# Two added ordering rules in a spectral layer with a feed-forward behind it, on one core: a segment's products behind a gate, and the down matmuls behind the next unit's gate

## The chip, the cores and the metric

The kernel runs on 1 core of one Trainium2 chip. The metric is the device time of one execution in microseconds (us), lower is better. In the profile the engines are PE (TensorE's matmuls), PEld (its weight loads), DVE (VectorE), ACT (ScalarE), POOL (GpSimd) and SP (which issues the DMAs).

## The reference

The input is x of 8 batches of 3008 positions by 256 channels. A Fourier layer is followed by a feed-forward layer over all 8 x 3008 = 24064 positions:

```
X = np.fft.rfft(x, axis=1)
Yr = Xr @ w_r - Xi @ w_i + b_r
Yi = Xr @ w_i + Xi @ w_r + b_i
Yr, Yi = soft threshold of both at 0.01
y = np.fft.irfft(Yr + 1j * Yi, n=3008, axis=1)
...
h = y.reshape(24064, 256) @ w_in          # 256 x 2048
g = h * np.clip(h + 3.0, 0.0, 6.0) / 6.0
out = g @ w_out                           # 2048 x 256
```

## The kernel before

**The spectral part.** The transform of 3008 = 64 x 47 points is cut in two. For each batch `stage1` multiplies by the 47-point table (L332), `middle` does the 64-point transforms, the channel mixing with w_r and w_i and the threshold, and the way back (L421, the w_r/w_i/w_m products that go through the helper line L137, L506), and `segment` does the last 47-point products (L558) from `qt`, which a DMA loads. Each batch has seven segments; segment (b, k) writes its part of `raw`, the input of the feed-forward, by two ACT copies (L566) and DVE additions (L568, L580). `prepare(c)` then makes from chunk c of 512 positions the operands `yb`, each split into a high and a low part (L130 on ACT, L131 on DVE or POOL).

**The feed-forward.** There are 47 chunks of 512 positions, and for each one 8 *units* (c, f), each with two of the 16 column blocks of w_in: 376 units, numbered from 0. A unit's product with w_in is done as seven smaller *blocks* instead of eight (a Strassen scheme). A block is three matmuls of 256 columns (low x high, high x low, high x high). They go to three PSUM tiles:

- `pb` (two buffers, so unit i and unit i+2 share one) takes blocks 1, 6, 7 and 4 in this order, one on top of the other. After each block ACT copies the running sum out: `p1`, `u2`, `u3` (L620), and after block 4 `h` (L654). The next block into this buffer has to wait for that copy.
- `pd` (one buffer) takes block 2, `pc` (one buffer) blocks 5 and 3. DVE adds each of them to one of the copies, into `h` (L625).

`phase_a` (blocks 2, 1), `phase_b` (6), `phase_c` (7, 5) and `phase_d` (4, 3) issue them. `gate(i)` is then one ACT activation `r` (L661, the gate's first ACT operation), one DVE operation (L663), the ACT cast that gives the high part of `gs` (L130) and the DVE subtraction that gives the low part (L131). `down(i, step)` issues twelve matmuls of 512 columns in four steps (L685): eight with the high part of `gs`, four with the low part, into `po0` and `po1`, which add up over the 8 units of a chunk. The program issues unit i's blocks, unit i-1's gate and unit i-3's down matmuls in one pass of its loop.

**What sets the order.** The program text gives only a priority. A scheduler goes through the whole program with modelled times when the kernel is built, and fixes the order of each engine's queue: what is ready earlier there can be put ahead of what stands earlier in the text. Each engine then works its queue in that order. Spectral work is spread among the units by `lay(g, n, first, last)`, which puts the n steps of a piece into slots between units `first` and `last`; for segment (b, k) these come from `begin[b, k]`, when its chunk is needed.

Of the kernel before, what the change touches and what calls it, by code (L numbers as in the profile page):

```python
# [13 lines left out]
AF = mybir.ActivationFunctionType  # L14
# [86 lines left out]
def spectral_ffn(ctx: ExitStack, tc: tile.TileContext, x, w_r, w_i, bias, w_in, w_out, f47, f64, g64, sgn, out):  # L101
    nc = tc.nc
# [11 lines left out]
    def space(shape, dt, name, tag=None):  # L114
        tag = tag or name
        return sb.tile(shape, dt, name=name, tag=tag, bufs=depth.get(tag, 1))
# [6 lines left out]
    def room(wide=False):  # L123
        if wide:
            return ps_b.tile([P, 512], F32, name="pb")
        return ps_a.tile([P, 512], F32, name="ps_a")

    def split(hi, lo, src, on=None):

        nc.scalar.copy(out=hi, in_=src)  # L130
        (on or nc.vector).tensor_tensor(out=lo, in0=src, in1=hi.bitcast(F32), op=ALU.subtract)  # L131
# [14 lines left out]
    def loaded(src, rows, cols, name, at=None):  # L146

        hi = const.tile([rows, cols], F32R, name=name + "_hi")
        lo = const.tile([rows, cols], F32R, name=name + "_lo")
        st = const.tile([rows, cols], F32, name=name + "_all") if at is None else at  # L150
        nc.sync.dma_start(out=st[:rows, :cols], in_=src)
        return hi, lo, st[:rows, :cols]
# [5 lines left out]
    nf = NFT // 2  # L158
    three = const.tile([P, 1], F32, name="three")
# [219 lines left out]
    with tc.issue_after(stores[-1].ins):  # L379
        r, k = [loaded(w, P, 2 * D, n, t) for w, n, t in ((w_r, "w_r", spare[7]), (w_i, "w_i", spare[8]))]  # L380
# [149 lines left out]
    def segment(b, k, tag="qt", aside=None):  # L530
        n1, n = SEGS[k]
        gr = 2 if n == 2 * J else 1
        rows = n // gr * NK
        w = n * NK
        t0 = b * S + n1 * N2
        qt = space([P, 2, 2, D], F32, "qt", tag)
        for cs in range(2):
            src = scr2[b][cs, n1 : n1 + n].rearrange("(g j) k d -> (j k) g d", g=gr)
            nc.sync.dma_start(out=qt[:rows, cs, :gr], in_=src)
        for c in range(t0 // T, (t0 + n * N2 - 1) // T + 1):  # L540
            if c not in raw:
                raw[c] = space([P, 2, T], F32, "raw")
        yield

        def places(at, size):

            done = 0
            while done < size:
                c, q = divmod(t0 + at + done, T)
                m = min(size - done, T - q)  # L550
                yield c, q, done, done + m
                done += m

        for dh in range(2):
            ps = room(bool(aside) and dh == 1)
            for cs in range(2):
                for g in range(gr):
                    nc.tensor.matmul(  # L558
                        out=ps[:, cs * w + g * rows : cs * w + (g + 1) * rows],
                        lhsT=qt[:rows, cs, g, dh * P : (dh + 1) * P],  # L560
                        rhs=f47_s[2][:rows, cs * R47 : cs * R47 + rows],
                        start=True,
                        stop=True,
                    )
            odd = space([P, 2 * R47], F32, "odd", aside or "xi")[:, :w]
            nc.scalar.copy(out=odd, in_=ps[:, w : 2 * w])  # L566
            for c, q, lo, hi in places(0, w):
                nc.vector.tensor_tensor(out=raw[c][:, dh, q : q + hi - lo], in0=ps[:, lo:hi], in1=odd[:, lo:hi], op=ALU.add)  # L568

            some = lambda a: a.rearrange("p (n q) -> p n q", q=NK)[:, :, 1:]  # L570
            m = NK - 1
            for c, q, lo, hi in places(w, n * m):
                while lo < hi:
                    row, col = divmod(lo, m)
                    if col == 0 and hi - lo >= m:
                        r1, c1 = hi // m, m
                    else:
                        r1, c1 = row + 1, min(m, col + hi - lo)
                    size = (r1 - row) * (c1 - col)
                    nc.vector.tensor_tensor(  # L580
                        out=raw[c][:, dh, q : q + size].rearrange("p (n q) -> p n q", n=r1 - row),
                        in0=some(ps[:, :w])[:, row:r1, col:c1],
                        in1=some(odd)[:, row:r1, col:c1],
                        op=ALU.subtract,
                    )
                    lo, q = lo + size, q + size
            yield
# [20 lines left out]
            yield  # L608

    units = [(c, f) for c in range(NC) for f in range(nf)]  # L610
    hs, ps_of, keep, gs, pos = {}, {}, {}, {}, {}

    def block(i, n, ps, start):
        c, f = units[i]
# [42 lines left out]
    def gate(i):  # L657

        h = hs.pop(i)
        r = space([P, 2, T], F32, "r")  # L660
        nc.scalar.activation(out=r, in_=h, func=AF.Relu, bias=three, scale=1.0)  # L661
        yield
        nc.vector.scalar_tensor_tensor(out=r, in0=r, scalar=6.0, in1=h, op0=ALU.min, op1=ALU.mult)  # L663
        t = gs[i] = space([P, 2, 2, T], F32R, "gs")
        split(t[:, 0], t[:, 1], r)
        yield
# [6 lines left out]
    )  # L673

    def down(i, step):

        c, f = units[i]
        g = gs[i]
        for u, dh, which, low in STEPS[step]:
            if f == 0 and step < 2 and u == 0 and which == "l":  # L680
                pos[dh] = ps_o.tile([P, 512], F32, name=f"po{dh}")
            part = int(f in shares[1])
            ft = 2 * (f - shares[part][0]) + u
            w = wout_s["hl".index(which)][part]
            nc.tensor.matmul(  # L685
                out=pos[dh],
                lhsT=w[:, ft * D + dh * P : ft * D + (dh + 1) * P],
                rhs=g[:, low, u],
                start=f == 0 and u == 0 and which == "l",
                stop=f == nf - 1 and u == 1 and low == 1,  # L690
            )
            if f == nf - 1 and u == 1 and low == 1:
                ot = space([P, T], F32, "ot")
                if dh:
                    nc.vector.tensor_scalar(out=ot, in0=pos[dh], scalar1=1.0 / 6.0, scalar2=None, op0=ALU.mult)
                else:
                    nc.scalar.mul(out=ot, in_=pos[dh], mul=1.0 / 6.0)
                nc.sync.dma_start(out=out[dh * P : (dh + 1) * P, c * T : (c + 1) * T], in_=ot)
# [16 lines left out]
    with tc.high_priority():  # L715
        for k, tag, aside in ((0, "qt", "p1"), (1, "h", "u2")):
            run(segment(0, k, tag, aside))
        run(prepare(0))
# [4 lines left out]
    def lay(g, n, first, last):  # L723

        q = -1
        for i in range(n):
            q = max(q + 1, int(4 * (first + (last - first) * i / n)))
            while q in taken:
                q += 1
            taken.add(q)  # L730
            slots.setdefault(q, []).append(g)
        return q / 4 + 0.5
# [3 lines left out]
    begin = {}  # L736
    for b in reversed(range(B)):
        for k in reversed(range(len(SEGS))):
            first = 8 * ((b * S + SEGS[k][0] * N2) // T)
# [8 lines left out]
    for b in range(B):  # L748
        for k in range(len(SEGS)):
            if (b, k) not in ((0, 0), (0, 1)):  # L750
                lay(segment(b, k), 3, max(0, begin[b, k]), max(3, begin[b, k] + 3))
        if b:
            lay(middle(b), 3 * (NK // 2) + 2, max(after, per * (b - 1) - 14), begin[b, 0] - 1.5)
        if 0 < b < B - 1:
            after = lay(stage1(b + 1), 29, max(after, per * (b - 1) - 10), max(15, per * b - 16))
# [13 lines left out]
    for i in range(n + 3):  # L769
        for kind, f in ((in_band, i), (out_band, i - 3)):  # L770
            while 0 <= f < nf and (kind, f) not in ready:
                turn(LATE)
        if i < n:
            phase_a(i)
        gated(i - 2)
        fill(4 * i)
        if 0 <= i - 3 < n:
            down(i - 3, 0)
        if 0 <= i - 1 < n:
            phase_c(i - 1)  # L780
        fill(4 * i + 1)
        if 0 <= i - 3 < n:
            down(i - 3, 1)
        if i < n:
            phase_b(i)
        fill(4 * i + 2)
        if 0 <= i - 3 < n:
            down(i - 3, 2)
        if 0 <= i - 1 < n:
            phase_d(i - 1)  # L790
            gates[i - 1] = gate(i - 1)
            gated(i - 1)
        fill(4 * i + 3)
        if 0 <= i - 3 < n:
            down(i - 3, 3)
            gs.pop(i - 3)
# [47 lines left out]
```

## Time and profile before

| | us |
|---|---|
| median of 3 runs | 2629.21 |
| lowest, highest | 2628.64, 2632.96 |
| profiled execution | 2629.63 |
| its span, first to last instruction | 2627.9 |
| PE busy / PEld busy | 2557.6 / 2282.9 |
| DVE / ACT / POOL busy | 1971.7 / 1814.5 / 764.8 |

The profiled execution lies 0.42 us above the median, and 1.7 us of its time lie outside the span. A matmul's bar in the timeline is longer than the distance to the next one's start (0.28 us against 0.12 us for 256 columns), since matmuls are pipelined. So short waits of PE hide under a "busy" bar; the distance of two starts shows them, and the idle time of PEld, whose weight load carries the wait, does too.

### The profile page before, as it was taken

The page shows a single profiled execution, that of the slowest core. Times are in us where ns is not written, and L with a number is a line of the kernel's source. Part 1 is how long each engine was busy: PE and PEld are TensorE (multiplying, and loading weights), DVE is VectorE, ACT ScalarE, POOL GpSimd, SP SyncE. Part 2 cuts the span into 40 slices and gives each one's busy share as a digit, 9 for nine tenths or more (in the row PEclk, how much of TensorE's full clock was granted, in tenths as well). Part 3 has the DMA queues.
Part 4 walks back from the last instruction along what each step waited for, and adds up shares of the span by engine and source line. Part 5 has one row for each costly group of instructions (what it writes and reads, how often), then busy time and mean ns, then how long its engine had stood idle before and what let it go on. Part 6 is the DMA issues. An engine that isn't in the chain of part 4 may idle for free.

```text
span 2627.9 us, 44428 instructions
## 1 busy us (share of the span) xinstructions
PE 2557.6 (97%) x16392; PEld 2282.9 (87%) x16392; DVE 1971.7 (75%) x3195; ACT 1814.5 (69%) x3578; POOL 764.8 (29%) x726
## 2 busy tenths in 40 slices
PE   5789999999999999999999999999999999999999
PEld 4578889988888888998898888988989889888887
DVE  7687777777778777877778777777777777666766
ACT  5477777777767676676766677767776666676666
POOL 3233332333323332333314243233321121131310
PEclk8989999999999999999999999999999999999999
DMA  8643422332123212222223222222222111100000
GB/s 263 186 127 90 114 83 81 88 88 69 56 85 89 78 58 64 87 86 82 62 65 92 74 65 74 80 75 80 66 76 60 48 58 50 41 29 27 12 17 17
DMA packets 149985, 199.97 MB, mean 76 GB/s; under 512 B 16847, under 2 KB 103751, under 8 KB 149767
## 3 DMA queue, kind: packets, MB, share of 16 engines
q1 hardware_dynamic: 149767, 197.13, 25.5%
q8 instruction: 129, 2.11, 0.3%
q14 instruction: 89, 0.73, 0.1%
HBM read 97.45 MB, written 74.97 MB: 66 GB/s over the span
## 4 chain that ended last, share of the span: by engine, by line
PE 84%; DVE 6%; ACT 4%; DMA 2%; issue 1%; SPq 0%; POOL 0%; ACTq 0%; DVEq 0%
PE po L685 37%; PE pb L137 17%; PE ps_a L137 10%; PE pc L137 9%; PE pd L137 4%; PE ps_a L558 3%; PE ps_a L421 2%; ACT gs L130 1%; ACT r L661 1%; DVE r L663 1%; DVE gs L131 1%; DVE h L625 1%; DVE tc L475 0%; DVE tc L474 0%; DMA zt<-tc 0%
## 5 line engine op out<-in xcount | busy, mean ns | idle before, releaser
L685 PE MATMUL po<-gs,w_out_hi 128*128 128x512 f32 x3008 | 1008.6, 396 | 0.0
L663 DVE SCALAR_TENSOR_TENSOR r<-r,h 128x1024 f32<-128x1024 f32 x376 | 486.4, 1294 | 253.2 <-ACT r L661 251.0
L685 PEld LDWEIGHTS po<-gs,w_out_hi 128*128 128x128 f32 x3008 | 540.4, 188 | 84.0
L685 PE MATMUL po<-gs,w_out_lo 128*128 128x512 f32 x1504 | 602.4, 401 | 4.8 <-ACT gs L130 2.3
L137 PE MATMUL pb<-yb,w_in_hi 128*128 128x256 f32 x3008 | 571.3, 279 | 1.3 <-DVE yb L131 1.3
L661 ACT ACTIVATE r<-h,three 128x1024 f32<-128x1024 f32 x376 | 434.7, 1156 | 197.9 <-DVE h L625 195.0
L131 DVE TENSOR_TENSOR gs<-r,gs 128x1024 fp32r<-128x1024 f32 x376 | 486.2, 1293 | 74.0 <-ACT gs L130 72.1
L137 PEld LDWEIGHTS pb<-yb,w_in_hi 128*128 128x128 f32 x3008 | 460.5, 189 | 19.9 <-DVE yb L131 1.6
L130 ACT CAST gs<-r 128x1024 fp32r<-128x1024 f32 x376 | 396.0, 1053 | 97.2 <-DVE r L663 93.8
L625 DVE TENSOR_TENSOR h<-pc,u 128x256 f32<-128x256 f32 x752 | 315.3, 419 | 182.7 <-PE pc L137 168.8
L131 POOL TENSOR_TENSOR yb<-T,yb 128x256 fp32r<-128x256 f32 x184 | 177.7, 971 | 904.8 <-ACT yb L130 870.3
L137 PE MATMUL pb<-yb,w_in_lo 128*128 128x256 f32 x1504 | 430.8, 288 | 5.9 <-ACT yb L130 2.3
L620 ACT COPY u<-pb 128x256 f32<-128x256 f32 x752 | 279.3, 374 | 113.3 <-PE pb L137 96.9
L685 PEld LDWEIGHTS po<-gs,w_out_lo 128*128 128x128 f32 x1504 | 282.7, 188 | 63.0 <-ACT gs L130 13.6
L137 PEld LDWEIGHTS pb<-yb,w_in_lo 128*128 128x128 f32 x1504 | 283.2, 189 | 30.2 <-ACT h L654 4.2
L137 PE MATMUL pc<-yb,w_in_hi 128*128 128x256 f32 x1504 | 296.8, 279 | 0.0
L137 PEld LDWEIGHTS pc<-yb,w_in_hi 128*128 128x128 f32 x1504 | 229.9, 188 | 12.0 <-DVE yb L131 0.3
L137 PE MATMUL pc<-yb,w_in_lo 128*128 128x256 f32 x752 | 218.0, 290 | 1.7 <-DVE h L625 1.5
L620 ACT COPY p<-pb 128x256 f32<-128x256 f32 x376 | 140.1, 373 | 67.4 <-PE pb L137 66.1
L654 ACT COPY h<-pb 128x256 f32<-128x256 f32 x376 | 140.9, 375 | 52.2 <-PE pb L137 51.0
L625 DVE TENSOR_TENSOR h<-pd,p 128x256 f32<-128x256 f32 x376 | 157.0, 418 | 19.4 <-ACT p L620 12.2
L137 PEld LDWEIGHTS pc<-yb,w_in_lo 128*128 128x128 f32 x752 | 141.6, 188 | 16.0 <-DVE h L625 3.5
(139 smaller groups left out, 3878.8 us busy)
## 6 DMA issues: line engine op xcount, KB each, us to landing
bt<-scr SPq DMA_DIRECT2D x96, 256.0 KB, 3.0
scr<-pt SPq DMA_DIRECT2D x96, 256.0 KB, 2.3
zt<-tc SPq DMA_DIRECT2D x376, 64.0 KB, 2.0
out<-ot SPq DMA_DIRECT2D x94, 256.0 KB, 2.3
scr<-a SPq DMA_DIRECT2D x96, 240.0 KB, 2.7
qt<-scr SPq DMA_DIRECT2D x96, 240.0 KB, 3.4
xin<-in_x SPq DMA_DIRECT2D x38, 480.0 KB, 4.5
f<-in_f SPq DMA_DIRECT2D x96, 128.0 KB, 2.8
```

The source lines that it names most:

```text
L130: nc.scalar.copy(out=hi, in_=src)
L131: (on or nc.vector).tensor_tensor(out=lo, in0=src, in1=hi.bitcast(F32), op=ALU.subtract)
L137: nc.tensor.matmul(out=ps, lhsT=a, rhs=b, start=start and n == 0, stop=stop and n == len(todo) - 1, skip_group_check=more,)
L421: nc.tensor.matmul(out=psv[:, dh, :, u, :], lhsT=data[:, u, dh * P : (dh + 1) * P], rhs=f[:, u, :], start=True, stop=True,)
L558: nc.tensor.matmul(out=ps[:, cs * w + g * rows : cs * w + (g + 1) * rows], lhsT=qt[:rows, cs, g, dh * P : (dh + 1) * P], rhs=f47_s[2][:row ...
L620: nc.scalar.copy(out=t, in_=ps)
L625: nc.vector.tensor_tensor(out=to, in0=ps, in1=keep.pop((i, n)), op=ALU.add)
L654: nc.scalar.copy(out=hs[i][:, 1, :H], in_=pb)
L661: nc.scalar.activation(out=r, in_=h, func=AF.Relu, bias=three, scale=1.0)
L663: nc.vector.scalar_tensor_tensor(out=r, in0=r, scalar=6.0, in1=h, op0=ALU.min, op1=ALU.mult)
L685: nc.tensor.matmul(out=pos[dh], lhsT=w[:, ft * D + dh * P : ft * D + (dh + 1) * P], rhs=g[:, low, u], start=f == 0 and u == 0 and which == ...
```

## The change

A function `ordered(later, earlier)` adds a dependency to the scheduler's graph that carries no semaphore (`NoSync`): the order of the queues has to obey it, no engine waits for it. It is used twice.

- The matmuls of the third segment of batch 0, (b, k) = (0, 2), are put behind the first ACT operation of unit 0's gate, and its three steps are laid between units 1.25 and 3.5 instead of 0 and 3.
- From unit 16 on, each down matmul of unit i is put behind the first ACT operation of unit i+1's gate.

```
+    def ordered(later, earlier):
+        why = mybir.DependencyInfo(mybir.DependencyClass.NoSync, mybir.DependencyReason.DATA)
+        tc.add_manual_dep(later.ins, earlier.ins.name, why, reason="order")
...
-                    nc.tensor.matmul(
+                    made_by = nc.tensor.matmul(
...
+                    if (b, k) == (0, 2):
+                        ordered(made_by, gated_by[0])
...
-        nc.scalar.activation(out=r, in_=h, func=AF.Relu, bias=three, scale=1.0)
+        gated_by[i] = nc.scalar.activation(out=r, in_=h, func=AF.Relu, bias=three, scale=1.0)
...
-            nc.tensor.matmul(
+            made_by = nc.tensor.matmul(
                 out=pos[dh],
...
+            if i + 1 in gated_by and i >= 2 * nf:
+                ordered(made_by, gated_by[i + 1])
...
-                lay(segment(b, k), 3, max(0, begin[b, k]), max(3, begin[b, k] + 3))
+                first, last = max(0, begin[b, k]), max(3, begin[b, k] + 3)
+                lay(segment(b, k), 3, *((1.25, 3.5) if (b, k) == (0, 2) else (first, last)))
```

No instruction is added or taken out. In the rows below, the number behind a name tells tiles apart.

PE at the start of the feed-forward, before: qt_1230 is segment (0, 2), pd_1207 and pb_1206 are unit 0.

```order
L558 MATMUL ps_a_1160<-f47_all_90,qt_1156 128x120 x4
L558 MATMUL pb_1170<-f47_all_90,qt_1156 128x120 x4
L558 MATMUL ps_a_1296<-f47_all_90,qt_1230 128x120 x4
L137 MATMUL pd_1207<-yb_1185,w_in_lo_79 128x256
L137 MATMUL pb_1206<-yb_1188,w_in_lo_79 128x256
L558 MATMUL ps_a_1376<-f47_all_90,qt_1230 128x120 x4
L137 MATMUL pb_1272<-yb_1188,w_in_lo_79 128x256
L137 MATMUL pd_1207<-yb_1185,w_in_hi_78 128x256 x2
```

The same place now:

```order
L558 MATMUL ps_a_1160<-f47_all_90,qt_1156 128x120 x4
L558 MATMUL pb_1170<-f47_all_90,qt_1156 128x120 x4
L137 MATMUL pd_1207<-yb_1185,w_in_lo_79 128x256
L137 MATMUL pb_1206<-yb_1188,w_in_lo_79 128x256
L137 MATMUL pb_1268<-yb_1188,w_in_lo_79 128x256
L137 MATMUL pd_1207<-yb_1185,w_in_hi_78 128x256 x2
```

The eight products of segment (0, 2) have gone; they stand some thirty rows later, behind all seven blocks of unit 0, and the first matmuls of `middle(1)` (L421), which stood between unit 0's blocks, stand behind unit 0's first eight down matmuls.

PE late in the program, before: pb_28449 is unit 349, pb_28567 unit 351, which takes the same PSUM buffer; gs_28521 is unit 348.

```order
L137 MATMUL pb_28449<-yb_28042,w_in_lo_79 128x256
L137 MATMUL pb_28449<-yb_28042,w_in_hi_78 128x256 x2
L137 MATMUL pd_28568<-yb_27889,w_in_lo_79 128x256
L137 MATMUL pd_28568<-yb_27889,w_in_hi_78 128x256 x2
L137 MATMUL pc_28530<-yb_28066,w_in_lo_79 128x256
L137 MATMUL pc_28530<-yb_28066,w_in_hi_78 128x256 x2
L685 MATMUL po0_28348<-gs_28521,w_out_lo1_1088 128x512
```

Now (the down matmuls that follow are those of unit 347, gs_28462):

```order
L137 MATMUL pb_28449<-yb_28042,w_in_lo_79 128x256
L137 MATMUL pb_28449<-yb_28042,w_in_hi_78 128x256 x2
L137 MATMUL pb_28567<-yb_27924,w_in_lo_79 128x256
L137 MATMUL pb_28567<-yb_27924,w_in_hi_78 128x256 x2
L137 MATMUL pd_28568<-yb_27889,w_in_lo_79 128x256
L137 MATMUL pd_28568<-yb_27889,w_in_hi_78 128x256 x2
L137 MATMUL pc_28530<-yb_28007,w_in_lo_79 128x256
L137 MATMUL pc_28530<-yb_28007,w_in_hi_78 128x256 x2
L691 MATMUL po0_28348<-gs_28462,w_out_lo1_1088 128x512
```

The down matmuls, which stood in groups of eight and four between the blocks, now stand twelve in a row and one unit later, and the blocks stand closer: the last block of unit 349 in its buffer and the first of unit 351 in the same one, with two blocks, eight down matmuls and one more block between them before, follow each other directly.

ACT at the same place, before: r_28503 and gs_28521 are unit 348, p1_28517 and u2_28546 unit 350, u3_28537 and h_28451 unit 349.

```order
L654 COPY h_28392<-pb_28390 128x256
L620 COPY u2_28487<-pb_28449 128x256
L661 ACTIVATE r_28503<-h_28392,three_75 128x1024
L620 COPY p1_28517<-pb_28508 128x256
L620 COPY u3_28537<-pb_28449 128x256
L130 CAST gs_28521<-r_28503 128x1024
L620 COPY u2_28546<-pb_28508 128x256
L654 COPY h_28451<-pb_28449 128x256
```

Now (r_28444 and gs_28462 are unit 347):

```order
L656 COPY h_28392<-pb_28390 128x256
L622 COPY u2_28487<-pb_28449 128x256
L663 ACTIVATE r_28444<-h_28329,three_75 128x1024
L130 CAST gs_28462<-r_28444 128x1024
L622 COPY p1_28517<-pb_28508 128x256
L622 COPY u3_28537<-pb_28449 128x256
L656 COPY h_28451<-pb_28449 128x256
L622 COPY u2_28546<-pb_28508 128x256
```

The copies `p1` and `u3`, which stood between the gate's two ACT operations, now stand behind both, and `gs` directly behind `r`.

## Rows read from the trace of the kernel before

**Rows 1.** The page's busy time of the engines with their share of the span, its slices of PE and of the granted clock (40 equal slices, tenths), and the engines' shares in the chain that ended last.

```profile
PE 2557.6 (97%) x16392; PEld 2282.9 (87%) x16392; DVE 1971.7 (75%) x3195; ACT 1814.5 (69%) x3578; POOL 764.8 (29%) x726
...
PE   5789999999999999999999999999999999999999
...
PEclk8989999999999999999999999999999999999999
...
PE 84%; DVE 6%; ACT 4%; DMA 2%; issue 1%; SPq 0%; POOL 0%; ACTq 0%; DVEq 0%
```

**Rows 2.** Busy time by stretch (us from the span's start: PE, PEld, DVE, ACT, POOL with instructions; then granted clock as a share of 2.4 GHz, DMA share, GB/s).

```profile
50.00:100.00 50.00, 37.34 (x256) 32.55 (x257) 41.07 (x70) 23.84 (x45) 13.23 (x14) 0.97 0.67 194
140.00:167.00 27.00, 17.30 (x88) 14.87 (x87) 26.42 (x56) 18.98 (x45) 12.54 (x13) 0.75 0.40 121
300.00:2390.00 2090.00, 2079.55 (x13508) 1873.45 (x13507) 1582.41 (x2563) 1467.33 (x2905) 625.90 (x578) 1.00 0.24 71
2390.00:2628.00 238.00, 231.61 (x1441) 205.32 (x1439) 160.15 (x240) 159.35 (x300) 45.18 (x49) 1.00 0.05 17
```

**Rows 3.** The start of the feed-forward in order of time (start us, us, engine line op, out<-in, count, and idle time before it with what released it): segment (0, 2)'s products, unit 0's blocks and the DVE's additions for that segment.

```profile
143.20 1.04 PE L558 MATMUL ps_a<-f_all,qt 120*128 120x120 f32 x4 [2.79 <-DMA qt<-scr]
145.02 1.21 PE L558 MATMUL ps_a<-f_all,qt 120*128 120x120 f32 x4 [0.78 <-DMA qt<-scr]
...
145.89 0.56 PE L137 MATMUL pd<-yb,w_in_lo 128*128 128x256 f32 x1
...
146.46 1.90 PE L558 MATMUL ps_a<-f_all,qt 120*128 120x120 f32 x8
...
147.63 0.23 DVE L568 TENSOR_TENSOR raw<-ps_a,odd 128x84 f32<-128x84 f32 x1
...
152.16 0.51 PE L137 MATMUL pb<-yb,w_in_lo 128*128 128x256 f32 x2 [2.29 <-ACT yb L130]
...
155.43 1.23 PE L137 MATMUL pb<-yb,w_in_hi 128*128 128x256 f32 x4 [1.34 <-DVE yb L131]
...
161.26 1.13 PE L421 MATMUL ps_a<-f,bt 128*128 128x128 f32 x8 [1.16 <-issue]
...
162.14 0.37 PE L137 MATMUL pc<-yb,w_in_lo 128*128 128x256 f32 x1
```

**Rows 4.** Who PE's weight loads waited for from 300 us to the end: us in total, times, longest.

```profile
PEld po L685 <- ACT gs L130: 13.6, 43, 1.2
PEld pb L137 <- ACT h L654: 3.8, 14, 0.3
PEld pb L137 <- ACT p L620: 3.1, 7, 0.9
PEld pc L137 <- DVE h L625: 2.8, 8, 0.5
PEld pd L137 <- DVE h L625: 2.1, 5, 1.0
PEld pb L137 <- ACT u L620: 1.5, 4, 0.7
```

**Rows 5.** One unit's start of a block on a buffer whose copy is not done, at 384 us: block 1, then block 6 of the same unit with only one other matmul's length between them in the order.

```profile
384.08 0.39 PE L137 MATMUL pb<-yb,w_in_hi 128*128 128x256 f32 x2
...
384.51 0.37 ACT L620 COPY p<-pb 128x256 f32<-128x256 f32 x1
...
384.94 0.39 PE L137 MATMUL pb<-yb,w_in_lo 128*128 128x256 f32 x1 [0.46 <-ACT p L620]
```

**Rows 6.** The same at 2040 us, with one block of another unit between: the last block of a unit, the other unit's block, and the first block of the unit that takes the first one's buffer.

```profile
2040.34 0.39 PE L137 MATMUL pb<-yb,w_in_hi 128*128 128x256 f32 x2
...
2040.57 0.28 PE L137 MATMUL pb<-yb,w_in_lo 128*128 128x256 f32 x1
...
2040.77 0.37 ACT L654 COPY h<-pb 128x256 f32<-128x256 f32 x1 [0.57 <-PE pb L137]
...
2041.19 0.38 PE L137 MATMUL pb<-yb,w_in_lo 128*128 128x256 f32 x1
```

**Rows 7.** ACT in one unit's time late in the program, in order of time.

```profile
2469.14 1.16 ACT L661 ACTIVATE r<-h,three 128x1024 f32<-128x1024 f32 x1 [1.15 <-DVE h L625]
2470.20 0.35 ACT L620 COPY u<-pb 128x256 f32<-128x256 f32 x1
2470.44 0.38 ACT L620 COPY p<-pb 128x256 f32<-128x256 f32 x1
2471.58 1.05 ACT L130 CAST gs<-r 128x1024 fp32r<-128x1024 f32 x1 [0.76 <-DVE r L663]
2472.54 0.36 ACT L654 COPY h<-pb 128x256 f32<-128x256 f32 x1
```

**Rows 8.** PE a little later: a block, the eight down matmuls before it, and the same group of the next unit.

```profile
2472.80 0.39 PE L685 MATMUL po<-gs,w_out_lo 128*128 128x512 f32 x1
2473.03 0.40 PE L685 MATMUL po<-gs,w_out_hi 128*128 128x512 f32 x1
...
2474.66 0.28 PE L137 MATMUL pb<-yb,w_in_lo 128*128 128x256 f32 x1
2474.78 0.39 PE L137 MATMUL pb<-yb,w_in_hi 128*128 128x256 f32 x2
2475.01 0.28 PE L137 MATMUL pb<-yb,w_in_lo 128*128 128x256 f32 x1
...
2477.98 0.39 PE L685 MATMUL po<-gs,w_out_lo 128*128 128x512 f32 x1
```

More of the change, by code (lines that the diff above doesn't have):

```diff
@@ L610, in spectral_ffn @@
     units = [(c, f) for c in range(NC) for f in range(nf)]
-    hs, ps_of, keep, gs, pos = {}, {}, {}, {}, {}
+    hs, ps_of, keep, gs, pos, gated_by = {}, {}, {}, {}, {}, {}
     def block(i, n, ps, start):
```

## The prediction

> **What bounds the kernel now.** I read first the page's busy times, slices and chain. PE is busy for 97% of the span, its share of the chain is 84%, and from the seventh slice of forty its slices are full at a granted clock of full speed [rows 1]. No work is taken out, so a time can come only from PE's waits. The stretches say where these lie: from 140 to 167 us PE is busy 17.3 of 27 us, at 0.75 of the clock; from 300 to 2390 us it is busy 2079.55 of 2090 [rows 2]. The second number hides short waits under the bars of pipelined matmuls, so I read next whom the weight loads waited for: of the waits after 300 us the largest item by far is the down matmuls on the cast of `gs`, 13.6 us in 43 waits; the waits of blocks on their copies and additions come to 13.3 us in 38 (3.8 + 3.1 + 2.8 + 2.1 + 1.5) [rows 4]. The change moves down matmuls back, so it is aimed at the first item, and it has to push blocks forward, which is the second.
>
> **Part 1, the third segment.** Before, its first product waits 2.79 and 0.78 us for its DMA while unit 0's first block stands behind it in PE's queue, and the eight products keep PE until 148 us with the clock down [rows 3]. That wait goes. What is late next is `yb`: PE then waits 2.29 us for the ACT cast and 1.34 us for the DVE subtraction [rows 3], and DVE is busy 26.42 of 27 us in this stretch [rows 2]. Only the DVE addition at 147.63 us (0.23 us) leaves that queue ahead of `yb`. Further on, L421 no longer stands in front of unit 0's last block, so PE's 1.16 us wait there and its run of 0.88 us (161.26 to 162.14) go [rows 3]: this block can start at about 162.14 - 1.16 - 0.88 - 0.25 = 159.85 us. But 16 segment passes and 8 of L421, some 0.11 us each at full clock, are then still to do: 2.7 us, so the comparable point is 162.5 us against 162.14. They fill small holes of unit 1's start (under 1 us). I take **-0.5 us**, with -2 and +1 as ends: all of the 2.29 us wait moved away, and nothing filled. On SP's queue the load of segment 3 goes behind two loads of `middle(1)`; its data are for chunk 2, which begins sixteen units in, and I cost that at nothing (a late arrival would cost a wait like the 2.79 us).
>
> **Part 2, the gain.** No wait is added by the rule itself, only order. I counted, for each unit from 17 on, the PE work that stands between the last matmul of its blocks and its first down matmul, a 256-column matmul at 0.116 us and a 512-column one at 0.232 us (2474.66 to 2474.78, 2472.80 to 2473.03) [rows 8]. What must happen in this time is a copy, `r`, a DVE operation and the cast: 0.32 us to the copy [rows 6], then from a late unit's row of ACT about 2.44 us from `r` to `gs` and 0.96 us of `gs`, with the copy and addition ahead some 4.3 us in all [rows 6, 7]. Before, the work between is 4.2 us or less in one unit of twenty and 5.8 us at the median; now it is 6.5 and 7.9 us. So nearly all of the 43 waits should go. Each also costs the first matmul its overlap, about 0.1 us (its bar is 0.39 us, not 0.28) [rows 5]. 13.6 + 4.3 = 17.9 us at most; some small waits on a queue that runs late will stay. I take **-15 us**, ends -18 and -8.
>
> **Part 2, the price.** The same count for blocks that need the copy or addition of an earlier block, over seven such pairs per unit. With no matmul between the two, PE starts the second 0.75 us after the first (the block's last matmul at 384.19, the next at 384.94) instead of 0.12 us [rows 5]; with the lost overlap that is 0.74 us. With one block between, 2040.45 to 2041.19 is again 0.74 us [rows 6], of which 0.47 is work: 0.27 + 0.11 = 0.38 us. With two blocks between, 0.82 us of work cover it and about 0.04 us are left, an estimate from these two rows. Pairs with under 0.3 us of work between: 1 before, 20 now. From 0.3 to 0.6 us: 26 before, 75 now. From 0.6 to 0.9 us: 37 before, 179 now. The difference is 19 x 0.74 + 49 x 0.38 + 142 x 0.04 = 14.1 + 18.6 + 5.7 = 38.4 us. A pair that lies around another's wait is paid with it; I take a tenth off: **+34 us**. The ends are +20 (two in five lie inside others) and +38.
>
> **Part 2, the queue on ACT.** Late in the program there is little spectral work to put between. There the order of ACT adds a second wait that the count does not hold: `p1` now stands behind `gs`, and `gs` behind `r` with a DVE operation between [rows 7]. I follow two units from the last matmul of unit 348's block 4, at 0. Its copy starts at 0.32, `u2` 0.25 later (2470.20 to 2470.44), `r` at 0.82, `gs` at 3.26 (2469.14 to 2471.58), `p1` at 4.22 (2471.58 to 2472.54) and PE's block 6 of unit 350, 0.42 after the copy's start (2040.77 to 2041.19), at 4.64 [rows 6, 7]. PE itself is there at 0.12 + 0.35 + 12 x 0.232 + 3 x 0.35 = 4.30 [rows 8]: 0.34 us of wait and 0.1 of overlap, 0.44 us. In the next unit `p1` comes in time and the direct pair of the second order rows costs 0.74 us. So two units lose 1.18 us, 0.6 per unit, where the count above gives, for the last 43 units (12, 14 and 50 pairs), 0.38 per unit. The difference is 0.22 x 43 = **+10 us**; ends 0 (the two waits run together) and +25 (the same also in other units whose `p1` or `u3` stands behind such a `gs`, about 56 more).
>
> Sum, against the profiled execution's 2629.6 us, 0.4 above the median: 2629.6 - 0.5 - 15 + 34 + 10 = **2658 us**, +1.1%. With all low ends 2629.6 - 2 - 18 + 20 + 0 = 2630, with all high ends 2629.6 + 1 - 8 + 38 + 25 = 2686.
>
> **The rivals.**
> (1) Faster: twelve down matmuls in a row give ACT and DVE 2.8 us without a new block, so they enter each group of blocks with nothing queued, and the 38 block waits of before go as the 43 down waits do: 2629.6 - 15 - 13 = 2602 if the close pairs cost nothing, 2613 with a quarter of the 38.4 us paid. It decides where a close pair costs under about 0.1 us. For it speaks that most block waits of before are short (0.35 us at the mean [rows 4]); against it that 0.74 us is made of a matmul's end, a copy and a hand-over, with ACT idle before the copy in the 2040 us case [rows 6], so no free ACT shortens it. 10%.
> (2) No change: half the close pairs lie inside each other's waits and the queue on ACT adds nothing; -15 and +15 to +19 cancel, 2625 to 2634. 12%.
> (3) Slower still: the queue behind `gs` bites throughout; every one of the 56 further units loses 0.44 us, +25, and prepare's casts, which stand between `r` and `gs` in some units, make it longer: about 2685 to 2695. 15%.
> (4) The clock falls in the late stretch. There PE would be idle about a tenth of the time, in pieces of 0.4 to 0.6 us. From 50 to 100 us PE is idle a quarter of the time and the granted clock is 0.97 [rows 2], so I give this 3%. If the level of 1.2 GHz held for a quarter of the last 238 us, half of that stretch's work would be lost: some 30 us more, about 2690.
> The Trainium skill, "TensorE: Matmul & The Clock Gate", section "A second HAM failure mode: psum-queue depth-cycling", describes this: a kernel that cycles through PSUM banks leaves PE idle for short moments so often that the clock goes up and down. By that rule the time is that of rival 4; the clock of 0.97 between 50 and 100 us does not bear it out at this share of idle time.
>
> **How the numbers follow.** The forecast of 2658 us has 60% (2640 to 2680), rivals 1 to 4 have 10, 12, 15 and 3%. A measurement of this kernel can tell about 0.2% (5 us) from no change. Faster by more than that is rival 1: 0.10; within it rival 2: 0.12; slower is the rest: 0.78. The range leaves out rival 1, half of rival 2 and the far tip of rivals 3 and 4: 2629 to 2688.
>
> **What would show it.** The waits of down matmuls on `gs` after 300 us should fall from 13.6 us to under 4; if not, part 2's gain is wrong. The waits of `pb` on the copies `h`, `p` and `u` should rise from 8.4 us to some 30 or more, mostly single waits of 0.3 to 0.6 us; if they stay under 15, the price is wrong and rival 1 or 2 holds. The last 238 us should get longer by about 20 us; if they do not, the followed pair of units is wrong. The granted clock should stay full after 170 us. At the start, the down matmuls of unit 0 should begin some us earlier, with PE's backlog at 170 us within 1 us of before. A wait of PE for a segment's DMA after 200 us would show that the moved load on SP costs something.

## The result, and the profile of the changed kernel

The changed kernel takes 2667.07 us (median of 4 runs, 2665.39 to 2667.65) against 2630.52 us for the kernel before (4 runs beside it): 1.0137 times as long, 95% interval 1.012 to 1.0155, 37 us more. The forecast was 2658 us in a range of 2629 to 2688. The profiled execution took 2667.35 us, its span is 2665.6 us; it is 37.7 us above the profiled execution of before.

The page of the changed kernel: busy times, slices, and the engines' shares in the chain that ended last. It is read against [rows 1].

```profile
PE 2579.1 (97%) x16392; PEld 2292.2 (86%) x16392; DVE 1964.8 (74%) x3195; ACT 1819.6 (68%) x3578; POOL 752.1 (28%) x726
...
PE   5789999999999999999999999999999999999998
...
PE 85%; DVE 6%; ACT 4%; DMA 1%; issue 1%; SPq 0%; POOL 0%; DVEq 0%; ACTq 0%; POOLq 0%
```

The page shows almost nothing of a loss of 37 us: PE's share is 97% as before, because bars of matmuls that wait for each other stretch and count as busy (2579.1 us for the same 16392 matmuls that had 2557.6). Only the last slice has fallen, from 9 to 8.

The stretches of the changed kernel (columns as in [rows 2]), the last one up to its own end:

```profile
140.00:167.00 27.00, 16.78 (x77) 14.26 (x76) 24.40 (x48) 18.32 (x42) 10.10 (x11) 0.62 0.31 93
300.00:2390.00 2090.00, 2075.29 (x13415) 1865.47 (x13415) 1559.02 (x2549) 1461.33 (x2892) 608.15 (x578) 1.00 0.24 71
2390.00:2666.00 276.00, 258.94 (x1545) 223.45 (x1543) 173.29 (x255) 171.71 (x317) 47.25 (x49) 1.00 0.04 15
```

From 300 to 2390 us PE got through 13415 matmuls where it did 13508 before; what is missing there is still to do behind 2390 us. There PE is idle for 17 of 276 us, 5 of them behind its last matmul and 2 in one wait, and the granted clock is 1.00 all the same.

Whom PE's weight loads waited for from 300 us to the end (us in total, times, longest), to be laid beside [rows 4]:

```profile
PEld pb L137 <- ACT h L656: 18.7, 35, 0.7
PEld pc L137 <- DVE h L627: 10.5, 22, 0.8
PEld pb L137 <- ACT p L622: 8.8, 33, 0.7
PEld pb L137 <- ACT u L622: 6.0, 20, 0.7
PEld pd L137 <- DVE h L627: 2.6, 9, 0.6
PEld po L691 <- ACT gs L130: 2.4, 1, 2.4
```

The item at which the change is aimed has gone: 43 waits of down matmuls on the cast of `gs`, 13.6 us, have become one, that of the very last unit. What stood below it has grown: the waits of blocks on copies and additions from 13.3 us in 38 to 46.6 us in 119. Where they lie is seen in the same view from 2200 us on, first of the kernel before, then of the changed one:

```profile
PEld po L685 <- ACT gs L130: 4.6, 13, 0.9
PEld pb L137 <- ACT h L654: 0.5, 2, 0.3
PEld pc L137 <- DVE h L625: 0.4, 1, 0.4
```

```profile
PEld pb L137 <- ACT h L656: 13.6, 26, 0.7
PEld pc L137 <- DVE h L627: 5.5, 11, 0.5
PEld pb L137 <- ACT p L622: 2.9, 10, 0.7
```

Of the 18.7 us on the copy `h`, 13.6 lie in the last sixth of the program. One such wait, in PE's timeline of the changed kernel (start us, us, engine line operation, tiles, and the idle time before it): a unit's block 4, and behind it the first block of the unit that takes its buffer.

```profile
2509.54 0.28 PE L137 MATMUL pb<-yb,w_in_lo 128*128 128x256 f32 x1
2509.66 0.39 PE L137 MATMUL pb<-yb,w_in_hi 128*128 128x256 f32 x2
2510.51 0.38 PE L137 MATMUL pb<-yb,w_in_lo 128*128 128x256 f32 x1 [0.46 <-ACT h L656]
2510.73 0.41 PE L137 MATMUL pb<-yb,w_in_hi 128*128 128x256 f32 x2
```

The last matmul of block 4 starts 0.12 us behind 2509.66, the next one 0.73 us after that; the one behind it comes 0.22 us later and not 0.12. This is the direct pair that the forecast priced at 0.74 us from [rows 5, 6]. ACT in the same time:

```profile
2505.25 1.16 ACT L663 ACTIVATE r<-h,three 128x1024 f32<-128x1024 f32 x1
2507.71 1.05 ACT L130 CAST gs<-r 128x1024 fp32r<-128x1024 f32 x1 [1.29 <-DVE r L665]
2508.66 0.36 ACT L622 COPY p<-pb 128x256 f32<-128x256 f32 x1
2508.99 0.37 ACT L622 COPY u<-pb 128x256 f32<-128x256 f32 x1
...
2510.08 0.37 ACT L656 COPY h<-pb 128x256 f32<-128x256 f32 x1 [0.41 <-PE pb L137]
```

`gs` follows `r` directly and ACT stands idle for 1.29 us in front of it, until the DVE operation is done; the copies `p` and `u` queue behind it. ACT itself was idle before the copy `h`: a free ACT does not shorten a direct pair.

**Lost time by place.** A sharper measure than the waits is the distance of matmul starts. For each matmul I took its distance from the one before, less 0.233 us for 512 columns before it, 0.116 for 256 and 0.111 for less, and added up what is over by more than 0.06 us, by the tile of the matmul that came late (`po` is the down matmuls). The stretches run from the cast of `gs` of one unit to that of another; all in us, one profile each. The wait for the last unit's `gs` lies behind them (0.7 us before, 2.1 in the changed kernel).

| kernel | units 16 to 304 | po / pb / pc / pd | units 304 to 375 | po / pb / pc / pd |
|---|---|---|---|---|
| before | 1944.2 | 17.5 / 15.4 / 8.8 / 3.1 | 392.8 | 4.9 / 1.7 / 1.2 / 0.6 |
| changed | 1951.4 | 2.0 / 32.1 / 11.7 / 4.2 | 422.5 | 0.7 / 24.0 / 8.0 / 1.1 |
| e3_downs_mid | 1951.0 | 2.1 / 32.7 / 12.3 / 4.1 | 392.3 | 3.2 / 2.6 / 1.8 / 0.5 |
| e4_downs_late | 1944.2 | 18.3 / 14.6 / 9.2 / 3.2 | 421.8 | 0.9 / 24.5 / 6.8 / 0.9 |
| e5_third | 1953.5 | 1.9 / 31.9 / 11.9 / 4.2 | 403.1 | 0.2 / 9.6 / 6.7 / 0.4 |
| e7_act_order | 1955.8 | 2.0 / 32.1 / 12.4 / 4.0 | 399.8 | 7.8 / 4.7 / 1.5 / 0.6 |
| e9_third_act | 1950.1 | 2.0 / 31.9 / 11.2 / 4.0 | 393.3 | 2.6 / 2.5 / 1.9 / 0.4 |
| e10_block3 | 1939.6 | 7.3 / 24.9 / 10.0 / 3.0 | 390.9 | 2.9 / 1.5 / 2.5 / 0.6 |
| e11_addition | 1929.2 | 6.2 / 11.6 / 13.7 / 0.6 | 396.6 | 2.0 / 2.1 / 5.8 / 0 |
| e12_mixed | 1932.5 | 7.3 / 13.2 / 13.8 / 0.6 | 392.0 | 3.0 / 1.2 / 3.0 / 0.5 |

Of the 37 us, 0.4 are there by unit 16, 7 come in the 288 units of the middle, 30 in the last 71 units. The cut at unit 304 is not sharp: e5_third, e7_act_order and e9_third_act have the rule of the changed kernel in the middle, and it reads 1950.1 to 1955.8 us there, so what the late edits do is better read from the run times.

### The profile page after: what moved, and what is told of

The parts are those of the page before. It is cut to its first block, busy times and chain, and to the rows that moved or that the text cites. A ratio compares the mean times of both kernels' runs of the same rounds, so it can differ in the third digit from the quotient of the medians.

```text
span 2665.6 us, 44603 instructions
## 1 busy us (share of the span) xinstructions
PE 2579.1 (97%) x16392; PEld 2292.2 (86%) x16392; DVE 1964.8 (74%) x3195; ACT 1819.6 (68%) x3578; POOL 752.1 (28%) x726
## 4 chain that ended last, share of the span: by engine, by line
PE 85%; DVE 6%; ACT 4%; DMA 1%; issue 1%; SPq 0%; POOL 0%; DVEq 0%; ACTq 0%; POOLq 0%
PE po L691 36%; PE pb L137 18%; PE ps_a L137 11%; PE pc L137 9%; PE pd L137 4%; PE ps_a L558 3%; PE ps_a L421 3%; DVE r L665 1%; DVE gs L131 1%; ACT gs L130 1%; DVE h L627 1%; ACT r L663 1%; ACT h L656 1%; DMA zt<-tc 0%; DVE tc L475 0%
## 5 line engine op out<-in xcount | busy, mean ns | idle before, releaser
L691 PE MATMUL po<-gs,w_out_hi 128*128 128x512 f32 x3008 | 954.5, 395 | 0.0
L691 PEld LDWEIGHTS po<-gs,w_out_hi 128*128 128x128 f32 x3008 | 561.3, 188 | 104.4
L691 PE MATMUL po<-gs,w_out_lo 128*128 128x512 f32 x1504 | 593.0, 394 | 2.2 <-ACT gs L130 2.0
L131 DVE TENSOR_TENSOR gs<-r,gs 128x1024 fp32r<-128x1024 f32 x376 | 478.6, 1273 | 143.1 <-ACT gs L130 141.3
L137 PE MATMUL pb<-yb,w_in_hi 128*128 128x256 f32 x3008 | 579.7, 280 | 1.0 <-DVE yb L131 1.0
L137 PE MATMUL pb<-yb,w_in_lo 128*128 128x256 f32 x1504 | 449.9, 300 | 20.6 <-ACT h L656 10.9
L131 POOL TENSOR_TENSOR yb<-T,yb 128x256 fp32r<-128x256 f32 x184 | 170.1, 932 | 951.6 <-ACT yb L130 932.1
L137 PEld LDWEIGHTS pc<-yb,w_in_hi 128*128 128x128 f32 x1504 | 243.5, 189 | 21.1 <-DVE yb L131 0.3
```

Of the source, the lines that this page charges most:

```text
L137: nc.tensor.matmul(out=ps, lhsT=a, rhs=b, start=start and n == 0, stop=stop and n == len(todo) - 1, skip_group_check=more,)
L691: made_by = nc.tensor.matmul(out=pos[dh], lhsT=w[:, ft * D + dh * P : ft * D + (dh + 1) * P], rhs=g[:, low, u], start=f == 0 and u == 0 an ...
```

## The experiments

Each time is the median of 4 to 11 runs, beside 9 to 21 runs of the kernel before with medians of 2629.6 to 2631.0 us.

**e1_segment and e2_downs: the two parts alone.** The first takes the down rule out of the changed kernel:

```
-            if i + 1 in gated_by and i >= 2 * nf:
-                ordered(made_by, gated_by[i + 1])
```

> Only the first part: the rule for segment (0, 2) and its later slots; no down matmul is bound. Theory A (the cost sits in the late units, where blocks follow each other closely): about +2 us on 2630.5, so 2632, because in the changed kernel PE waited 3.62 us for the cast of yb at 145 us with nothing to do and the low clock then lasted about 14 us in one piece more than before. Theory B (the prediction on record): -0.5 us, 2630. Theory C (a mere shift of the start that the rest of the program takes up): 2630.5, with the lag at 170 us of about 2 us gone by 300 us.

Measured: 2634.77 us, 1.0011 (1.0002 to 1.002), 3 to 4 us more. The second keeps the down rule and takes out the rule and the slots of segment (0, 2):

```
-                    if (b, k) == (0, 2):
-                        ordered(made_by, gated_by[0])
...
-                lay(segment(b, k), 3, *((1.25, 3.5) if (b, k) == (0, 2) else (first, last)))
+                lay(segment(b, k), 3, first, last)
```

> Only the second part: from unit 16 on each down matmul behind the next unit's gate; segment (0, 2) as before. Theory A: +34 us on 2630.5, so 2664 to 2666, all but about 2 us of the change. Theory B (the prediction on record, by its sum of -15 + 34 + 10): +29, 2659. Theory C (the two parts act on each other, since a PE that is late at the start leaves the pairs closer): clearly under 2660.

Measured: 2667.63 us, 1.0141 (1.0125 to 1.0156). So the down rule carries the whole change; with it, the segment part makes no difference (2667.07 with, 2667.63 without). For e1_segment theory A has the sign, but not the reason. Its profile is 1.0 us behind that of before at unit 16 and 5.7 us at unit 76; in between (420 to 720 us) stands, in the view of weight-load waits,

```profile
PEld ps_a L558 <- ACT X L130: 2.1, 1, 2.1
```

a single wait of a segment's product. Whether that explains 3 us in eleven runs stays open. Nor is the low clock at the start a matter of the segment: in the stretch from 140 to 167 us e2_downs and e4_downs_late, whose order there is that of before, show

```profile
140.00:167.00 27.00, 18.06 (x89) 16.42 (x88) 25.01 (x52) 18.56 (x45) 13.73 (x15) 0.62 0.44 129
```

```profile
140.00:167.00 27.00, 18.35 (x88) 16.44 (x88) 24.69 (x51) 18.44 (x44) 14.25 (x17) 0.63 0.46 142
```

a granted clock of 0.62 and 0.63, like the changed kernel, where the kernel before shows 0.75 [rows 2].

**e3_downs_mid and e4_downs_late: the down rule by stretch.** Both are e2_downs with another condition:

```
-            if i + 1 in gated_by and i >= 2 * nf:
+            if i + 1 in gated_by and 2 * nf <= i < 304:     # e3_downs_mid
+            if i + 1 in gated_by and i >= 304:              # e4_downs_late
```

> The down rule for units 16 to 303 alone; segment (0, 2) and the units from 304 on are ordered as before. Theory A: in the middle the waits on the cast of gs that go (about 9 us visible of 13.6) and the close pairs that come (about 10 us of new visible waits) nearly cancel, +3 to +6 us, 2634 to 2636. Theory B (the rule costs everywhere the same per unit, and what is lost in the middle only shows late because work is pushed back): 288 of 360 units, about +27, 2657. Theory C (the gain of the middle is real and the price is late alone): -10, 2620.

> The down rule for units 304 to 375 alone; segment (0, 2) and units 16 to 303 are ordered as before. Theory A: nearly all of the price, +28 to +32 us, 2659 to 2662, 0.45 us per unit, with the waits of pb on the copy h after 2200 us at about 13 us as in the changed kernel. Theory B (the same cost per unit everywhere): 72 of 360 units, +7, 2637. Theory C (the late cost is work that the middle pushes back): near 2630.

Measured: 2639.85 us, 1.0033 (1.0021 to 1.0044), and 2659.65 us, 1.0111 (1.0097 to 1.0125). The two, +8.9 and +28.7 us, add up to 37.6, which is about the +36.7 of e2_downs. So nothing is pushed from the middle into the late stretch: the price there arises there, 0.4 us per unit. In the middle the rule does what it says, 15 us fewer are lost before down matmuls, and 17 us more before `pb`, 3 to 4 before `pc`, 1 before `pd`. Theories B and C of both fall. The middle's net of +9 is above the +3 to +6 that I expected; in the profiles it is 7.

**e5_third and e6_before_third: room for the copy.** From unit 304 on every third unit takes its `pb` from the pool of the spectral part, in the changed kernel and in the one before:

```
-        pb = ps_b.tile([P, 512], F32, name="pb")[:, :H]
+        third = i >= 304 and i % 3 == 2
+        pb = (ps_a.tile([P, 512], F32, name="pb", tag="ps_a") if third else ps_b.tile([P, 512], F32, name="pb"))[:, :H]
```

> The changed kernel, with every third unit's pb from unit 304 on in the PSUM room of the spectral part (ps_a), so that the copy h of a unit has longer before its buffer is needed. In the order, direct pairs of a unit's last block and the next first block in its buffer (under 0.6 us of work between) fall from 34 to 10 after unit 300; gs still follows r directly on ACT in 20 late units, as before in 22. Theory A (the close pairs on pb are the price): by the prices of the prediction (0.74, 0.38 and 0.04 us) the late price falls from 22 to 9 us, so 2667 - 13 = 2654, and the waits of pb on the copy h after 2200 us fall from 13.6 to about 4 us. Theory B (the queue on ACT, with p1 and u3 behind gs, is the price): no more than 4 us gained, 2663 or more. Theory C (a busier ps_a makes the segments wait): slower than 2667.

> The kernel before with the same third place for pb from unit 304 on and no rule. It tells what the third place does by itself. Theory A: few block waits on the copy h are there to be cured (0.5 us after 2200 us), the down matmuls on gs keep their 4.7 us: 2630.5 +- 3. Theory C: the segments wait for room in ps_a, +5 or more.

Measured: 2647.77 us (1.0068, 1.0056 to 1.0081), 19 us less than the changed kernel, and 2635.62 us (1.0021, 1.0012 to 1.003), 5 us more than before. The waits of e5_third from 2200 us on:

```profile
PEld pc L137 <- DVE h L627: 5.4, 13, 0.9
PEld pb L137 <- ACT h L657: 3.7, 8, 0.7
PEld pb L137 <- ACT u L622: 2.9, 9, 0.4
...
PEld pb L137 <- ACT p L622: 0.2, 1, 0.2
```

The waits on `h` fell from 13.6 to 3.7 us, as theory A had it, and those on `p` nearly vanished too (0.2 us for 2.9), so the gain is larger than 13. Theory B falls: with `p1` and `u3` still mostly behind `gs` on ACT, two thirds of the late price are gone. Those of `pc` on the additions have stayed. In e6_before_third the cost is not where theory C put it (at `ps_a`) but at `pc`, 4.8 us after 2200 us: in its order 13 of the units 331 to 373 have their blocks 5 and 3 in `pc` with less than 0.9 us of work between, and none in that of before.

**e7_act_order, e8_two_first, e9_third_act: the order on ACT, and one block between.** e7_act_order binds the cast in the changed kernel (`cast_of` holds the cast of each unit's `gs`):

```
+            made_by = nc.scalar.copy(out=t, in_=ps)
+        for m, late in (("p1", 3), ("u3", 2)):
+            if n == m and i - late in cast_of and i >= 304:
+                ordered(cast_of[i - late], made_by)
```

> The changed kernel, and from unit 304 on the cast of gs of unit i is put behind the copies p1 of unit i+3 and u3 of unit i+2 on ACT, so that no such copy stands behind a cast that waits for DVE. The down rule stays. The order that comes out has no direct pair under 0.3 us after unit 300 (16 in the changed kernel) and 4 under 0.6 (23). Theory A (close pairs): 2667 - 18 = 2649. Theory A with the queue on ACT as the second part of the price, as predicted: 2667 - 28 = 2639, the level of the kernel with the rule in the middle alone. Theory B (twelve down matmuls in a row, or gs that comes a unit later, is what costs): 2665 or more, with waits of the down matmuls on gs.

Measured: 2646.99 us (1.0066, 1.0054 to 1.0079), 20 us less than the changed kernel. From 2200 us on its waits are

```profile
PEld po L695 <- ACT gs L670: 7.6, 15, 1.2
PEld pb L137 <- ACT u L622: 1.4, 5, 0.4
...
PEld pc L137 <- DVE h L630: 1.3, 3, 0.5
PEld pb L137 <- ACT p L622: 1.0, 4, 0.3
```

Both kinds of block waits are gone, those of `pc` too, and the cast, pushed back, is waited for again: the time is that of close pairs alone, for a reason that neither line of theory A named. As the expectation says, this order also leaves no direct pair late, so the run does not separate the queue on ACT from the close pairs. e8_two_first puts one block between (the last argument puts the matmuls of block 1 behind the first of block 2):

```
-        block(i, 2, pd, True)
-        block(i, 1, pb, True)
+        first = block(i, 2, pd, True)
+        block(i, 1, pb, True, first if i >= 304 else None)
```

> The changed kernel, and from unit 304 on block 1 of each unit is put behind the first matmul of its block 2, so that a block stands between the last block of a unit and the first of the next in its buffer. Direct pairs under 0.3 us fall from 16 to 4 after unit 300, those of 0.3 to 0.6 us from 23 to 17; ACT's order keeps gs directly behind r. Theory A (close pairs): the late price falls from 22 to 13 us, 2667 - 9 = 2658. Theory B (the queue on ACT): no gain, 2664 to 2668.

Measured: 2661.36 us (1.012, 1.0104 to 1.0135), 6 us less. The waits on `h` fell to 3.5 us, as in e5_third, but `pd` now waits for its addition, from 2200 us on

```profile
PEld pd L137 <- DVE h L630: 4.4, 10, 0.6
PEld pb L137 <- ACT p L625: 3.6, 13, 0.8
PEld pb L137 <- ACT h L659: 3.5, 8, 0.7
```

4.4 us where it was 0.7. The time lies between the two theories. e9_third_act joins the edits of e5_third and e7_act_order.

> The changed kernel with both late cures at once, from unit 304 on: every third unit's pb in ps_a, and the cast of gs behind the copies p1 and u3 on ACT. Each alone gave about 2647, some 20 us better than the changed kernel and some 7 us worse than the rule in the middle alone (2639.85). Theory A (the price is close pairs plus the queue on ACT, and each cure removes the pairs): what the third place left is the queue (waits of pc on the additions h, 5.4 us after 2200 us), what the ACT order left are waits on gs; both together about 2641, with the waits of pc under 2 us. Theory B (what is left is the twelve down matmuls in a row, which neither touches): 2647 again.

Measured: 2636.13 us (1.0021, 1.0012 to 1.003), 31 us less than the changed kernel, with a late stretch of 393.3 us for 392.8 before. From 2200 us on:

```profile
PEld po L696 <- ACT gs L671: 3.2, 8, 1.3
PEld pc L137 <- DVE h L630: 1.5, 4, 0.5
...
PEld pb L137 <- ACT h L660: 0.8, 3, 0.3
```

The time is 5 us below theory A's, and the waits of `pc` are under 2 us as it said. Theory B's premise did not hold: the order on ACT splits the rows of twelve down matmuls, which stand late in the trace 55 times in the changed kernel, 53 times in e5_third, 26 times in e7_act_order and 13 times here. Against theory B speaks e5_third, which keeps 53 of them and gives 19 us back, and e11_addition below, which has 130 in the middle and is faster there; that the rows cost a part of the 10 us that e5_third still loses late is not excluded. By the run times the third place alone gives 19 us, the order on ACT alone 20, both 31: the two overlap, and no run tells what each would be by itself.

**e10_block3, e11_addition, e12_mixed: a weaker rule.** In the kernel before, the down matmuls of unit i are put behind the last matmul of block 3 of unit i+1 (e10_block3), or behind its DVE addition (e11_addition), both ahead of that unit's `r`, which the change uses. `last` holds the last matmul of each block and the addition, `ordered` is that of the change:

```
+            behind = (i + 1, 3)                              # e10_block3
+            behind = (i + 1, "z")                            # e11_addition: "z" is the addition of block 3
+            behind = (i + 1, "z" if i < 304 else 3)          # e12_mixed
+            if behind in last and i >= 16:
+                ordered(made_by, last[behind])
```

> The kernel before with a weaker rule from unit 16 on: the down matmuls of unit i behind the last matmul of block 3 of unit i+1, instead of behind the gate's first ACT operation of unit i+1. In its order the work between a unit's blocks and its first down matmul is never under 5.0 us (before: 3.8), and the close pairs are no more than before (under 0.3 us: 0 for 1; 0.3 to 0.6: 21 for 26). Theory A (the gain is in the waits on gs, the price in the close pairs, and they can be had apart): of about 22 us lost before the first down matmuls, waits included, two thirds go and nothing comes: 2630 - 14 = 2616, between 2612 and 2622. Theory B (the waits on gs are only where PE catches up with ACT and DVE, and come back at the next block): 2627 to 2632, with the waits of blocks up by what the down matmuls lose.

> The same, one step later: the down matmuls of unit i behind the DVE addition of block 3 of unit i+1, which is the last operation ahead of that unit's gate. The close pairs fall in the middle (0.3 to 0.6 us: 7 units for 23) and rise late (0.6 to 0.9 us: 42 for 3, 0.3 to 0.6: 2 for 3); the least work ahead of a first down matmul is 5.0 us and the short ones are fewer. Theory A: 2630 - 18 + 1 = 2613, between 2609 and 2620. Theory B (the waits come back): 2627 to 2632. Theory C (a down matmul that comes later than its time costs by itself, as the rule of the change does): between this and 2667, so 2640 or more.

Measured: 2624.21 us (0.9978, 0.9969 to 0.9987) and 2620.94 us (0.9961, 0.9949 to 0.9974). Both are faster than the kernel before, by 7 and 10 us, both by less than theory A gave. For e10_block3 theory B is half right: 10 us less are lost before the down matmuls of the middle, 9.5 more before `pb`; the stretch gets only 4.6 us shorter. With e11_addition the middle gains 15 us, since `pb` loses less as well (11.6 for 15.4), and the late stretch loses 4 at `pc`. That asks for the later rule in the middle and the earlier one late.

> The kernel before with the later of the two weak rules in the middle (units 16 to 303: down matmuls of unit i behind the DVE addition of block 3 of unit i+1) and the earlier one late (from unit 304: behind the last matmul of that block 3). In the profiles the addition rule gained 14 us from unit 16 to 296 and lost 4 us from 304 on, the block rule lost nothing late. In the order, the close pairs after unit 304 fall from 44 to 5. Theory A (late, the close pairs decide): 2621 - 5 = 2616, between 2612 and 2619. Theory B (the late loss of the addition rule is no matter of the order): 2621 again.

Measured: 2617.01 us (0.9952, 0.9939 to 0.9966), 12.6 us less than before, as theory A had it; the fastest version of the study. Its waits from 300 us on, for [rows 4]:

```profile
PEld pc L137 <- DVE h L626: 5.4, 11, 0.9
PEld po L692 <- ACT gs L130: 4.8, 14, 0.9
PEld pb L137 <- ACT p L621: 3.4, 11, 0.6
```

The waits on `gs` are down to 4.8 us from 13.6. Those on `p` are at 3.4 for 3.1; of the waits of blocks, those of `pc` have grown most, 5.4 for 2.8.

## Why the prediction was right, and where its terms were off

The forecast of slower, its mechanism and its range held; 2658 us was 9 us too low. The signs that it named came too: the waits on `gs` fell to 2.4 us, those of `pb` on its copies rose from 8.4 to 33.5 us in 88 waits, the last 43 units took 18 us longer for about 20, and the clock stayed full from 170 us to PE's last matmul. That the sum came so close is in part luck, since errors of both signs stand in it.

**Part 1, -0.5 us.** The wait for the segment's DMA went, as said, and its successor is what the forecast named. PE's start of the feed-forward in the changed kernel:

```profile
145.00 0.58 PE L137 MATMUL pd<-yb,w_in_lo 128*128 128x256 f32 x1 [3.62 <-ACT yb L130]
...
147.23 0.55 PE L137 MATMUL pb<-yb,w_in_lo 128*128 128x256 f32 x1 [1.34 <-DVE raw L582]
...
152.99 0.80 PE L137 MATMUL pb<-yb,w_in_lo 128*128 128x256 f32 x2 [2.94 <-ACT yb L130]
```

PE comes earlier to `yb` and waits longer for it, 3.62 and 2.94 us where it waited 2.79 for the DMA and 2.29 for `yb` [rows 3]. Unit 0's down matmuls begin at 168.1 us for 169.8, and by unit 16 the profile is 0.4 us behind: nothing, within what a profile shows. By itself the part cost 3 to 4 us in e1_segment and beside the down rule nothing; why it cost anything stays open. No wait for a segment's DMA came of the moved load near it.

**Part 2, the gain, -15 us.** Before the down matmuls 22.4 us were lost (17.5 + 4.9), now 2.7 (2.0 + 0.7): -19.7, more than the 17.9 that the sum called the most. It was worked out from the waits of weight loads, 13.6 us and 4.3 for overlap, and these did not hold all that was lost.

**The price of close pairs, +34, and the queue on ACT, +10.** Blocks lose 50 us more by the same measure (pb 39, pc 9.7, pd 1.6): this term was too small, by 6 us. Another 7 us of the 37 lie outside both items, some 4 of them in distances too small for the measure. So the miss of 9 us is some 13 us of price that the sum lacked, less 5 us of gain that it lacked too. The direct pair measured 0.73 us for 0.74. How the 50 us divide between close pairs and the queue on ACT is not shown: the order on ACT, added to the third place, gives 12 us by the run times, near the 10 of the forecast, but alone it gives 20, since it also moves the pairs apart. `pc` loses 8.0 us late for 1.2, though few of its own pairs stand close (11 under 0.9 us of work from unit 304 on, for 4 before): it waits for an addition of DVE that needs the copy `u3` or `u2`. In e7_act_order, where `u3` stands ahead of `gs`, 1.5 us are lost there; the forecast had `u3` behind `gs` in its high end alone. The followed units had lost 0.6 us each by the working; over the units 304 to 375 it is 0.42 net, and 0.48 without the gain on `gs`.

**Middle and end.** The sum did not say where the time would be lost. Taken by stretch the same count gives it: close pairs of +17 us against the gain of 15 in the middle, +22 and 10 late, where the gain is 4. e4_downs_late (+29) is near the late sum of +28; e3_downs_mid (+9) is not the +2 of the middle. There the gain was as forecast (15 us less lost before the down matmuls), but the blocks cost 21 to 22 us for 17.

**The rivals.** Rival 1 (a close pair costs under 0.1 us) and rival 2 fell with the 46.6 us of block waits (with a quarter of the price paid rival 1's own sum is 2611, not 2613). In e11_addition and e12_mixed, where the pairs stay apart, blocks do lose less than before at `pb`, so a small part of rival 1's reasoning is sound. Rival 3 is excluded by its size, 2685 us and more, and by e3_downs_mid: in the middle the queue does not bite throughout, though the waits on `p` from 300 to 2200 us rose from 3.1 us in 7 to 5.9 in 23; that the spectral work between the blocks covers it there is likely, but was not tried by itself. Rival 4 did not come: up to its last matmul PE is idle for 12 of the last 271 us, 2 of them in one wait and the rest in pieces of under 0.6 us, and the granted clock there is 1.00. The rule of the Trainium skill, "TensorE: Matmul & The Clock Gate", section "A second HAM failure mode: psum-queue depth-cycling", would have had it go up and down; no stretch from 300 us on shows that here. The 0.97 from 50 to 100 us, which the prediction took against this rival, is weaker evidence than it looked: it holds a short fall of the clock, 0.57 from 78 to 82 us.

## What to carry to other kernels

An order rule that keeps one consumer from waiting moves other work forward, and each pair of accumulations that shares a buffer and comes closer pays a whole hand-over through the engine that empties it; count those pairs by stretch, because the price of the same rule can differ widely: here it was 0.03 us per unit in the middle and 0.4 late, where little spectral work is left to put between (that this is the reason was not tried). Bind to the earliest operation that still gives the slack needed: one operation earlier (the last addition ahead of the gate instead of the gate's first operation) turned +37 us into -10, and the +29 late into -1 to -2 where the bound was the matmul before it. A page that says 97% before and after can hide this; the distances of matmul starts, summed by the tile that came late, show it.

## What was not expected of the hardware

The granted clock at the start of the feed-forward differs between profiles of kernels whose order there is the same: 0.75 before, 0.62, 0.81 and 0.63 in e2_downs, e3_downs_mid and e4_downs_late from 140 to 167 us. By unit 2 their profiles stand 2.6, 3.2 and 3.4 us behind that of before, the one at 0.81 about as far as the two at 0.62 and 0.63, so a term of a few us at this place can't be read from one profile.
